# Block products for the second product of a second pair of token tiles, with its block weights made ahead

## Chip, cores and metric

One NeuronCore of a Trainium2 chip runs the whole program. The metric is the device time in microseconds (us) of one execution; the median of the runs shown counts.

## What is computed

Linear attention with an RMS norm feeds two MLPs, all in float32. There are 4608 tokens, a model width of 512, and inner widths of 2048 and 768.

```python
kv  = einsum('bhsd,bhse->bhde', k, v)          # 8 batches, 8 heads, 576 tokens, head size 64
out = einsum('bhsd,bhde->bhse', q, kv)
x   = out / sqrt(mean(out*out) + 1e-6) * g_norm
g   = s * maximum(x @ w_in, 0)**2 + b          # first MLP:  512 -> 2048 -> 512
x   = g @ w_out
h   = maximum(maximum(x @ w1, x @ w2), x @ w3) # second MLP: 512 -> 768 -> 512
y   = h @ w_out2
```

## The kernel before

Every operand of a matmul is held as a high and a low part, and a product is three matmuls (high by high, high by low, low by high) that add up in a PSUM bank. ScalarE makes the high part by a copy, VectorE the low part by a subtraction. Tokens come in nine tiles of 512. Tiles 0 to 2 go through the first MLP in the classic form, beside attention. Tiles 3 to 8 go in three pairs, `PAIRS` = (3,4), (5,6), (7,8), called pair 1, 2 and 3 here (`s` = 0, 1, 2 in the code). Then the second MLP takes the tiles in super steps of one or two tiles.

**Block products.** Two tiles and two row chunks of a weight make a 2 by 2 block matrix, which is multiplied with seven block products instead of eight (`A11` to `S4`, `t1` to `t4`; products p1 to p7, later ones add to the bank of an earlier one after ScalarE has copied it). The first product of every pair (`h_steps`, eight steps `q` of 42 matmuls, 336 in all) and the whole second MLP (`v1`, nine block products; `Output`) have this form. The second product of the first MLP is classic in pairs 1 and 2: while step `q` of the first product runs, the four output chunks of tile `ta` take the gated rows of step `q - 1` (192 matmuls), rows of tile `tb` are stored to DRAM (`g_dr`), and class `Second` multiplies them afterwards (192 more, the run part). Only pair 3, `BLOCK_Y`, has it in block form, in class `Blocks` (line 1687): `beside` multiplies b11 and b21 beside the steps (96 matmuls), `sink` (1711) makes the operands t1 to t4 of a step by four subtractions on VectorE, `early` and `ready` load and split them, and `run` (1781) multiplies the five other products, eight each (240 matmuls).

**Weights.** `block_op(q)` (1630) adds high and low of two chunks of `w_out`, forms four combinations, splits them (four copies of 128x256 on ScalarE; two 128x512 and eight 128x256 operations on VectorE) and stores four results and one old block to `ws_dr`. The eight run beside the first product of pair 3. `fetch` (1699) brings them back, seven blocks (1792 KB) a time, into the two buffers `wa`; the last five go into a tile of their own, `cp`. `com_op(i)` makes the combined weights of block product i of the second MLP from two raw chunks (`fused`: on ScalarE two Abs, two scalings and four copies; on VectorE sixteen operations) and stores 1792 KB to `wc_dr[i]`; `out_op` does the same for the last product. Before, com_op 0 runs in the plain stage (line 1484), 1 and 2 beside tile 2 (1541), 3 in pair 1, 4 to 7 and `out_op(2)` in pair 2, and out_op 0, 1 and com_op 8 inside the first super step of the second MLP (1910).

**What sets the order.** The kernel is written as one program; `tick` counts matmuls, and `beside_of(fns, a, b)` spreads side work (attention for the next pair, weight operations, loads of the next tokens) evenly over a range of that count. A string such as "L....hr.hrs.ab..e..." says at which of equal steps a weight operation loads, computes and stores. `in_order` puts an instruction behind the main work's last one on its engine. From there a scheduler orders ready instructions of each engine; in the second MLP matmuls are tied to program order. All loads and stores go through SP's queue, in order, and `store` delays one by some ticks. A pool such as `wpo` (16 tiles for `w_out`) or `wa` (two) gives a tile again once its last reader is through.

Of the kernel before, what the change touches and what calls it, by code (L numbers as in the profile page):

```python
# [10 lines left out]
F32 = mybir.dt.float32  # L11
# [11 lines left out]
P = 128  # L23
# [48 lines left out]
def fused_kernel(ctx, tc, qt, kv, kvr, g_norm, w_in, w_out, s, b, w1, w2, w3, w_out2, out):  # L72
# [72 lines left out]
    BLOCK_Y = {len(PAIRS) - 1}  # L145
    ws_dr = dram.tile([5 * QF, P, 2, HW], F32, name="ws_dr")

# [422 lines left out]

    def four(nm):
        return w2p["p"].tile([P, 2 * DM], U32, tag="p", name=nm)

    def work(nm):
        return w2p["p"].tile([P, 2 * DM], U32, tag="p", name=nm)
# [26 lines left out]
    def fused(srcs, turned, target, dst, raws=None, tabs=wide, his=hi_tile):  # L602
# [59 lines left out]
        if target:  # L662
            def both(k):
                to_hi(k + 1)
                to_lo(k)

            fns += [partial(to_hi, 0), partial(both, 0), partial(both, 1), partial(to_lo, 2), end]
        else:
            fns += [partial(to_hi, *range(4)), partial(to_lo, *range(4)), end]
# [188 lines left out]
    def v1(si, q, w):  # L858
# [49 lines left out]
        a = copy(bank("a"), x)  # L908
        d = bank("d")
# [559 lines left out]

    def com_op(i, here=False, **homes):  # L1470
# [8 lines left out]
    homes = {  # L1479
        "raws": lambda: rawp.tile([P, 2 * DM], U32, tag="raw", name="raw"),  # L1480
        "tabs": lambda: [wt1.tile([P, DM], U32, tag="ta", name="tab") for _ in range(2)],
        "his": lambda: stage().bitcast(F32R).rearrange("p (n c) -> p n c", c=HW),
    }
    early = phased(com_op(0, **homes), "L.h.r.h.rs.a.b.e")
# [56 lines left out]
    seq = [fn for i in (1, 2) for fn in phased(com_op(i, **homes), "L..hrhrs.ab.e..")]  # L1541
    beside_of(seq, 0, 5 * len(seq))
# [87 lines left out]
    def block_op(q):  # L1630
        got = {}

        def sums():
            got["raw"], got["com"] = raw, com = blocks(four("F")), blocks(work("G"))
            for i in range(2):
                hi, lo = (wo[2 * q + i][:, z].bitcast(F32).rearrange("p (n c) -> p n c", c=HW) for z in range(2))
                nc.vector.tensor_tensor(out=raw[:, 2 * i:2 * i + 2], in0=hi, in1=lo, op=ALU.add)

            def tt(o, x, y, op):
                nc.vector.tensor_tensor(out=com[:, o], in0=x, in1=y, op=op)  # L1640

            tt(0, raw[:, 1], raw[:, 3], ALU.add)
            tt(1, com[:, 0], raw[:, 0], ALU.subtract)
            tt(2, raw[:, 2], com[:, 1], ALU.subtract)
            tt(3, raw[:, 0], raw[:, 1], ALU.subtract)

        def his():
            own = got["raw"].bitcast(F32R)
            for k in range(4):
                t = w2p["f"].tile([P, 2, HW], F32R, tag="f", name="ws") if k < 2 else own[:, 2 * k - 4:2 * k - 2]  # L1650
                got[k] = t
                nc.scalar.activation(out=t[:, 0], in_=got["com"][:, k], func=ACTF.Copy)

        def los():
            for k, to in enumerate((2, 0, 4, 1)):
                t = got[k]
                nc.vector.tensor_tensor(out=t[:, 1], in0=got["com"][:, k], in1=t[:, 0].bitcast(F32), op=ALU.subtract)
                store(ws_dr[to * QF + q], t.bitcast(F32), 12)
            with tc.issue_after(behind[0]):
                dma(out=ws_dr[3 * QF + q], in_=wo[2 * q + 1][:, :, HW:].bitcast(F32))  # L1660

        return [partial(tied_in, fn) for fn in (sums, his, los)]

# [23 lines left out]
    class Blocks:  # L1687


        def __init__(self, ta, tb):  # L1690
            self.ta, self.tb = ta, tb
# [3 lines left out]
            for q in range(QF):  # L1695
                self.w["b11", q], self.w["b21", q] = wo[2 * q], wo[2 * q + 1]
            self.made = 0

        def fetch(self, c):
            ks = list(range(7 * c, min(7 * c + 7, 5 * QF)))  # L1700
            if len(ks) == 7:
                t = wc_tile("wa").rearrange("p a b c -> p (a b c)").rearrange("p (k z c) -> p k z c", z=2, c=HW)
                got = [(ks, t)]
            else:
                got = [(ks, w2p["cp"].tile([P, 5, 2, HW], F32R, tag="hl", name="ws"))]
            for k, t in got:
                dma(out=t.bitcast(F32), in_=ws_dr[k[0]:k[-1] + 1].rearrange("k p z c -> p k z c"))
                for i in range(len(k)):
                    self.w[self.order[k[i]]] = t[:, i]

        def sink(self, q):
            r = self.raw
            a, b = ((wpo if q else w2p["g4"]).tile([P, 2, DM], F32, tag="w", name="ops") for _ in range(2))
            for nm, t in (("t1", a[:, 0]), ("t2", a[:, 1]), ("t3", b[:, 0]), ("t4", b[:, 1])):
                r[nm, q] = t

            def sub(nm, x, y):
                nc.vector.tensor_tensor(out=r[nm, q], in0=x, in1=y, op=ALU.subtract)

            def sink(i, j, x):  # L1720
# [13 lines left out]
        def early(self, cnt):  # L1734
            r = self.raw
            for nm, q in self.order[:cnt]:
# [44 lines left out]
        def run(self):  # L1781
            for k, e in enumerate(self.order):
# [230 lines left out]
```

## Time and profile before

| | us |
|---|---|
| median of 3 runs (1382.25 to 1385.03) | 1382.88 |
| the profiled execution: span, first to last instruction | 1383.6 |
| the profiled execution: its own time | 1385.45 |
| PE busy (matmuls) | 1358.9 |
| VectorE (DVE) busy | 986.8 |
| ScalarE (ACT) busy | 786.9 |

PE is TensorE's matmuls and PEld its weight loads, which overlap them; DVE is VectorE, ACT is ScalarE, and SP issues the transfers. The profile names a group of instructions by line, engine, operation and tiles, out<-in. The granted clock of TensorE was 0.998 of full speed on average, so every stretch here is at the level of 2.4 GHz.

### The profile page before, as it was taken

Reading aid. Unit: us, or ns where it says so; the run is one execution under the profiler, and the core shown is the slowest. Engines: PE = TensorE matmul, PEld = TensorE weight load, DVE = VectorE, ACT = ScalarE, POOL = GpSimd, SP = SyncE. Lnnn points to the kernel's source line nnn. Section 1 sums busy time; section 2 is a strip of 40 time slices with the busy share of each in tenths; the row PEclk is TensorE's granted clock in tenths of the full one; section 3 lists DMA queues with packets and bytes.
Section 4 is the critical chain, followed back from the end, with each engine's and each line's share of the span. In section 5 each row is a group of like instructions: output and inputs, shape, how many; then the busy total and the mean of one; then the engine's idle time right before and its main releaser. Section 6 shows DMA issues by size and latency. Waiting matters only on the chain.

```text
span 1383.6 us, 19615 instructions
## 1 busy us (share of the span) xinstructions
PE 1358.9 (98%) x6822; PEld 1122.2 (81%) x6822; DVE 986.8 (71%) x1878; ACT 786.9 (57%) x1538; POOL 10.6 (1%) x40
## 2 busy tenths in 40 slices
PE   8999999999999999999999999999999999999998
PEld 6878788787888888877887777887998888888886
DVE  8998887878767676678767676786684674666555
ACT  7975666666777657677466774444453442443332
POOL 1000000000000000000000000000000000000000
PEclk9999999999999999999999999999999999999999
DMA  8486647786666676786767979647865554563532
GB/s 305 127 250 210 213 146 224 258 294 233 242 241 233 202 298 225 270 303 221 278 219 245 325 261 332 239 157 260 307 236 173 199 197 152 185 249 114 176 144 62
DMA packets 140458, 311.43 MB, mean 225 GB/s; under 512 B 50118, under 2 KB 71750, under 8 KB 131398
## 3 DMA queue, kind: packets, MB, share of 16 engines
q1 hardware_dynamic: 140352, 310.17, 64.4%
q8 instruction: 54, 0.88, 0.3%
q14 instruction: 46, 0.38, 0.1%
q10 hardware_dynamic: 6, 0.00, 0.0%
HBM read 218.89 MB, written 91.23 MB: 224 GB/s over the span
## 4 chain that ended last, share of the span: by engine, by line
PE 76%; DMA 9%; DVE 8%; ACT 3%; issue 2%; SPq 1%; DVEq 0%; ACTq 0%
PE x L524 19%; PE y L524 16%; PE d L524 12%; PE o L524 9%; PE b L524 6%; PE a L524 6%; PE h L449 2%; DVE tb L155 2%; DMA wc_dr<-raw 1%; PE h L155 1%; DMA wq<-wo_dr 1%; PE ops L369 1%; DMA raw<-in_w_out 1%; PE y L155 1%; PE kvps L347 1%
## 5 line engine op out<-in xcount | busy, mean ns | idle before, releaser
L524 PE MATMUL y<-gh,w 128*128 128x512 f32 x720 | 236.6, 391 | 0.9 <-ACT gh L506 0.9
L524 PE MATMUL d<-t,wc 128*128 128x512 f32 (+1 forms) x828 | 199.5, 376 | 0.0
L524 PE MATMUL x<-t,wc 128*128 128x512 f32 (+1 forms) x828 | 199.3, 376 | 0.0
L524 PEld LDWEIGHTS d<-t,wc 128*128 128x128 f32 x828 | 148.7, 188 | 27.9
L524 PEld LDWEIGHTS x<-t,wc 128*128 128x128 f32 x828 | 148.4, 188 | 27.6
L524 PEld LDWEIGHTS y<-gh,w 128*128 128x128 f32 x720 | 135.1, 188 | 28.6 <-ACT gh L506 1.3
L524 PE MATMUL y<-gl,w 128*128 128x512 f32 x360 | 141.0, 392 | 0.7 <-DVE gl L507 0.7
L873 DVE TENSOR_TENSOR c<-d,u 128x512 f32<-128x512 f32 (+1 forms) x45 | 28.7, 637 | 116.3 <-PE d L524 115.8
L524 PE MATMUL x<-b,wc 128*128 128x512 f32 (+1 forms) x414 | 100.1, 377 | 2.5 <-DVE r L490 1.7
L524 PE MATMUL b<-b,wc 128*128 128x512 f32 (+1 forms) x414 | 100.3, 378 | 0.0
L524 PE MATMUL a<-b,wc 128*128 128x512 f32 (+1 forms) x414 | 100.3, 376 | 0.0
L524 PEld LDWEIGHTS x<-b,wc 128*128 128x128 f32 x414 | 74.2, 188 | 17.5 <-DVE r L490 2.7
L524 PEld LDWEIGHTS b<-b,wc 128*128 128x128 f32 x414 | 73.8, 188 | 15.7 <-ACT b L809 2.2
L524 PEld LDWEIGHTS a<-b,wc 128*128 128x128 f32 x414 | 74.3, 188 | 13.8
L524 PEld LDWEIGHTS y<-gl,w 128*128 128x128 f32 x360 | 67.7, 188 | 13.7 <-DVE gl L507 1.1
L524 PE MATMUL o<-t,wq 128*128 128x512 f32 (+1 forms) x354 | 75.5, 369 | 0.0
L155 PE MATMUL h<-xh,w 128*128 128x512 f32 (+1 forms) x216 | 73.3, 383 | 1.0 <-ACT r L155 0.9
L868 ACT ACTIVATE a<-x 128x512 f32<-128x512 f32 (+1 forms) x45 | 24.3, 539 | 86.5 <-PE x L524 86.4
L524 PEld LDWEIGHTS o<-t,wq 128*128 128x128 f32 x354 | 62.4, 188 | 11.2
L868 ACT ACTIVATE b<-x 128x512 f32<-128x512 f32 (+1 forms) x45 | 24.3, 539 | 77.2 <-PE x L524 77.2
L155 PE MATMUL y<-gh,w 128*128 128x512 f32 (+1 forms) x200 | 65.1, 371 | 0.8 <-ACT st L155 0.8
L507 DVE SCALAR_TENSOR_TENSOR gl<-r,cst,gh 128x512 fp32r<-128x512 f32 x56 | 41.9, 749 | 32.8 <-ACT gh L506 32.3
(243 smaller groups left out, 2679.0 us busy)
## 6 DMA issues: line engine op xcount, KB each, us to landing
wc<-wc_dr SPq DMA_DIRECT2D x44, 1792.0 KB, 7.5
wc<-wp_dr SPq DMA_DIRECT2D x16, 1792.0 KB, 8.3
kv<-in_kv SPq DMA_DIRECT2D x32, 512.0 KB, 5.7
wp_dr<-wc SPq DMA_DIRECT2D x8, 1792.0 KB, 6.7
raw<-in_w_out SPq DMA_DIRECT2D x23, 512.0 KB, 5.0
gb<-g_dr SPq DMA_DIRECT2D x46, 256.0 KB, 5.9
g_dr<-r SPq DMA_DIRECT2D x43, 256.0 KB, 2.2
y_dr<-st SPq DMA_DIRECT2D x42, 256.0 KB, 2.8
```

Of the source, the lines that this page charges most:

```text
L155: tail[eng] = call(*args, **kw).ins
L347: nc.tensor.matmul(pb[d, i * D:(i + 1) * D], lhsT=t[:, 0, d], rhs=t[:, 1, d], start=(c == 0), stop=(c == NC))
L369: nc.tensor.matmul(pb, lhsT=l, rhs=r, start=(i == 0), stop=(i == 2))
L449: nc.tensor.matmul(h[:, :n], lhsT=w[:, z, kk, :], rhs=x[:, kk, o:o + n], start=(i == 0), stop=(i == 3 * KD - 1))
L507: nc.vector.scalar_tensor_tensor(out=gl, in0=r, scalar=b, in1=gh.bitcast(F32), op0=ALU.add, op1=ALU.subtract).ins,
L524: ins = nc.tensor.matmul(*args, **kw)
L868: main["act"] = nc.scalar.activation(out=out, in_=pb, func=ACTF.Copy).ins
L873: main["dve"] = nc.vector.tensor_tensor(out=o, in0=pb, in1=t, op=ALU.add).ins
```

## The change

Pair 2 joins pair 3 in `BLOCK_Y`. The eight block-weight operations move from pair 3 to earlier stages: 0 and 1 in the plain stage, 2 to 5 beside tile 2, 6 and 7 in the run part of pair 1. They also store the blocks b11 and b21 to `aw_dr`, from which pair 3 loads them again, since pair 2's operands take the places of `w_out`. The operations of the second MLP's weights move back: com_op 0 to pair 1, 1 and 2 to pair 2, 3 to 6 and out_op 2 to pair 3, 7 and 8 into the first super step, where a product now has seven places for side work instead of six. In pair 2 the four operands of the first step have no tiles that last; they go to DRAM (`op_dr`) and are loaded again. All 40 blocks now come through the two buffers `wa` (5 first, then 7 a time), and the first loads of what follows wait for a free one. In a block pair the side work must end with the first product (`T`). A second pool, `p2`, holds side work in pair 3. The core of the diff:

```diff
-    BLOCK_Y = {len(PAIRS) - 1}
+    BLOCK_Y = {len(PAIRS) - 2, len(PAIRS) - 1}
+    aw_dr = [dram.tile([P, 2, 2, HW], F32, name=f"aw_dr{q}") for q in range(QF)]
+    op_dr = [dram.tile([P, TW], F32, name=f"op_dr{i}") for i in range(4)]
...
     def four(nm):
-        return w2p["p"].tile([P, 2 * DM], U32, tag="p", name=nm)
+        taken[0] += 1
+        more = "p2" in w2p and taken[0] % 5 > 2
+        return w2p["p2" if more else "p"].tile([P, 2 * DM], U32, tag="p", name=nm)
...
         a = copy(bank("a"), x)
+        go()
         d = bank("d")
...
+        def end():
+            for k, to in enumerate((2, 0, 4, 1)):
+                dma(out=ws_dr[to * QF + q], in_=got[k].bitcast(F32))
+            with tc.issue_after(behind[0]):
+                for i in range(2):
+                    dma(out=aw_dr[q][:, :, i], in_=wo[2 * q + i][:, :, :HW].bitcast(F32))
+                dma(out=ws_dr[3 * QF + q], in_=wo[2 * q + 1][:, :, HW:].bitcast(F32))
...
-    early = phased(com_op(0, **homes), "L.h.r.h.rs.a.b.e")
+    early = [fn for q in range(2) for fn in phased(block_op(q, **taus), ".shl.e..")]
...
-    seq = [fn for i in (1, 2) for fn in phased(com_op(i, **homes), "L..hrhrs.ab.e..")]
-    beside_of(seq, 0, 5 * len(seq))
+    seq = [fn for q in range(2, 6) for fn in phased(block_op(q, **taus), ".shl.e..")]
+    beside_of(seq, 0, 6 * len(seq))
...
+        def weights(self, q):
+            if q < QF and ("b11", q) not in self.w:
+                t = wpo.tile([P, 2, DM], F32R, tag="w", name="w2")
+                with tc.issue_after(behind[0]):
+                    dma(out=t.bitcast(F32).rearrange("p z (i c) -> p z i c", i=2), in_=aw_dr[q])
+                self.w["b11", q], self.w["b21", q] = t[:, :, :HW], t[:, :, HW:]
+
+        CUTS = (0, 5, 12, 19, 26, 33, 40)
+
         def fetch(self, c):
...
+            a, e = self.CUTS[c:c + 2]
+            t = wc_tile("wa").rearrange("p a b c -> p (a b c)").rearrange("p (k z c) -> p k z c", z=2, c=HW)[:, :e - a]
+            with tc.issue_after(behind[0]):
+                dma(out=t.bitcast(F32), in_=ws_dr[a:e].rearrange("k p z c -> p k z c"))
...
+                own = [fpool("op") for _ in names]
+                self.away.update({(nm, q): op_dr[i] for i, nm in enumerate(names)})
...
             def sub(nm, x, y):
-                nc.vector.tensor_tensor(out=r[nm, q], in0=x, in1=y, op=ALU.subtract)
+                nc.vector.tensor_tensor(out=here[nm], in0=x, in1=y, op=ALU.subtract)
+                if (nm, q) in self.away:
+                    store(self.away[nm, q], here[nm], 8)
...
-                if k % 7 == 0 and 0 < k < 35:
...
+                if k in self.CUTS[1:5]:
+                    self.fetch(self.CUTS.index(k) + 1)
+                elif k == self.CUTS[5]:
+                    following(0)
...
+            following(1)
             self.out("b", self.tb, 0)
...
+        T = V + 12 * QF if blk else V + U
         if s + 1 < len(PAIRS):
-            beside_of(rare_steps(*groups[5 + s]), 0, V + U - 10)
+            beside_of(rare_steps(*groups[5 + s]), 0, T - 10)
         if s == 1:
-            ops = [com_op(i) for i in range(4, NQ - 1)] + [out_op(KC - 1)]
-            beside_of([fn for op in ops for fn in phased(op, "L....hr.hrs.ab..e...")], 0, V + U - 12)
+            beside_of([fn for i in (1, 2) for fn in phased(com_op(i), "L....hr.hrs.ab..e...")], 0, T - 12)
         if s == 2:
...
+            ops = [com_op(i) for i in range(3, NQ - 2)] + [out_op(KC - 1)]
+            beside_of([fn for op in ops for fn in phased(op, "L....hr.hrs.ab.e..")], 0, T - 12)
...
-                beside_of(phased(com_op(3), "L....hr.hrs.ab..e"), 20, 20 + 17 * 9)
+                beside_of(phased(com_op(0), "L....hr.hrs.ab..e"), 20, 20 + 17 * 9)
...
+        if s == 0:
+            beside_of([fn for q in (6, 7) for fn in phased(block_op(q), "shl..e..")], 115, U - 12)
...
-    ops = [out_op(0, True), out_op(1, True), com_op(NQ - 1, True)]
-    inside += [fn for op in ops for fn in phased(op, "L...hr.hrs.aaabe")]
+    ops = [out_op(0, True), out_op(1, True), com_op(NQ - 2, True), com_op(NQ - 1, True)]
+    inside += [fn for op in ops for fn in phased(op, "L..hr.hrs.aaab")]
```

## Rows read from the trace of the kernel before

**Rows 1.** Page, first part: engine, busy time, share of the span, instructions

```profile
PE 1358.9 (98%) x6822; PEld 1122.2 (81%) x6822; DVE 986.8 (71%) x1878; ACT 786.9 (57%) x1538; POOL 10.6 (1%) x40
```

**Rows 2.** Timeline of PE, begin of the second MLP: start, length, group

```profile
856.24 1.52 PE L524 MATMUL x<-b,wc 128*128 128x512 f32 x6
857.60 1.52 PE L524 MATMUL d<-t,wc 128*128 128x512 f32 x6
```

**Rows 3.** Timeline of PE, borders of pair 2, pair 3 and its run part

```profile
508.88 1.52 PE L524 MATMUL x<-b,wc 128*128 128x512 f32 x6
...
518.87 1.52 PE L524 MATMUL d<-t,wc 128*128 128x512 f32 x6
...
696.47 1.52 PE L524 MATMUL x<-b,wc 128*128 128x512 f32 x6
...
799.86 0.50 PE L524 MATMUL x<-gh,wc 128*128 128x512 f32 x1 [0.36 <-ACT keep L548]
```

**Rows 4.** Timeline of PE, attention's matmuls in pair 1 and pair 2

```profile
454.86 1.39 PE L347 MATMUL kvps<-kv 128*64 128x64 f32 x40
...
643.33 0.30 PE L369 MATMUL ops<-qh,kvbd 128*128 128x320 f32 x1
...
643.77 0.39 PE L524 MATMUL y<-gh,w 128*128 128x512 f32 x1
```

**Rows 5.** Waits of weight loads, 697 to 798: total, times, longest

```profile
PEld x L524 <- DVE r L490: 2.7, 3, 1.8
...
PEld b L524 <- ACT b L809: 1.7, 7, 0.4
```

**Rows 6.** Stretches: us, busy PE, PEld, DVE, ACT, POOL, clock, DMA share, GB/s

```profile
336.00:353.00 17.00, 17.00 (x78) 13.78 (x77) 12.40 (x22) 14.06 (x29) 0.00 (x0) 1.00 0.38 136
335.00:473.00 138.00, 138.00 (x767) 113.43 (x766) 94.89 (x180) 100.11 (x204) 2.41 (x8) 1.00 0.61 215
483.00:494.00 11.00, 11.00 (x50) 9.09 (x50) 10.88 (x21) 8.12 (x15) 0.00 (x0) 1.00 1.03 412
505.00:519.00 14.00, 14.00 (x64) 11.64 (x63) 8.61 (x14) 6.84 (x13) 0.00 (x0) 1.00 0.41 156
519.00:653.00 134.00, 131.66 (x661) 107.44 (x660) 98.46 (x202) 96.27 (x193) 0.61 (x2) 1.00 0.72 256
697.00:800.00 103.00, 100.64 (x432) 79.45 (x431) 70.62 (x139) 73.37 (x134) 0.00 (x0) 1.00 0.76 265
800.00:857.00 57.00, 56.02 (x244) 45.51 (x245) 43.50 (x69) 34.49 (x59) 0.00 (x0) 1.00 0.88 307
857.00:935.00 78.00, 78.00 (x346) 64.59 (x345) 59.74 (x121) 35.99 (x61) 0.00 (x0) 1.00 0.59 215
```

**Rows 7.** Groups of ACT, 516 to 655, the last 697 to 798: busy, mean ns, idle

```profile
L194 ACT ACTIVATE tab<-raw 128x512 f32<-128x512 f32 x10 | 6.7, 667 | 2.3 <-DMA raw<-in_w 1.4 <-DMA raw<-in_w_out 0.8 <-DVE raw L213 0.2
...
L409 ACT ACTIVATE y<-mps,cst 128x320 f32<-128x320 f32 (+1 forms) x12 | 6.1, 507 | 5.0 <-PE mps L407 4.9
...
L371 ACT ACTIVATE sq<-ops 128x320 f32<-128x320 f32 (+1 forms) x11 | 4.5, 413 | 1.5 <-PE ops L369 1.5
...
L643 ACT ACTIVATE hi<-raw 128x512 fp32r<-128x512 f32 x5 | 3.2, 631 | 4.0 <-DVE raw L213 4.0
...
L1652 ACT ACTIVATE ws<-G 128x256 fp32r<-128x256 f32 x16 | 6.2, 411 | 5.8 <-DVE G L1640 5.8
```

**Rows 8.** Groups of DVE, 516 to 655, the last two 697 to 798

```profile
L412 DVE SCALAR_TENSOR_TENSOR t<-t,y 128x320 f32<-128x320 f32 (+1 forms) x12 | 5.6, 465 | 0.2
...
L1637 DVE TENSOR_TENSOR F<-w 128x512 f32<-128x512 f32 x14 | 9.0, 683 | 0.0
...
L1657 DVE TENSOR_TENSOR ws<-G,ws 128x256 fp32r<-128x256 f32 x16 | 6.2, 416 | 0.0
```

**Rows 9.** DMA issues, whole span: count, size, median us to landing

```profile
wc<-ws_dr SPq DMA_DIRECT2D x5, 1792.0 KB, 8.6
...
ws<-ws_dr SPq DMA_DIRECT2D x1, 1280.0 KB, 10.7
```

More of the change, by code (lines that the diff above doesn't have):

```diff
@@ L665, in both, with close @@
                 to_lo(k)
[L667 removed]
+            def close():
+                to_lo(2)
+                end()
+            fns += [partial(to_hi, 0), partial(both, 0), partial(both, 1), close]
         else:
@@ L1477, in com_op @@
         return fused([chunk(ws[jb], mb), chunk(ws[ja], ma)], False, target if here else None, wc_dr[i], **homes)
[L1479 to L1483, printed above, removed]
-    early = phased(com_op(0, **homes), "L.h.r.h.rs.a.b.e")
+    taus = {"raws": lambda: rawp.tile([P, 2 * DM], U32, tag="raw", name="raw"), "ws": lambda: wt1.tile([P, DM], U32, tag="ta", name="ws").bitcast(F32R).rearrange("p (z c) -> p z c", z=2)}
+    early = [fn for q in range(2) for fn in phased(block_op(q, **taus), ".shl.e..")]
     todo, span, k_done, base = [], 1, 0, 0
@@ L1628, in out_op @@
         return fused([chunk(w_out2, 2 * c + k) for k in range(2)], True, target if here else None, wo_dr.get(c))
[L1630 to L1662, printed above, removed]
     prep.todo += [pair_op(i) for i in range(QF)]
@@ L1687, in fused_kernel, with __init__ @@
     class Blocks:
-        def __init__(self, ta, tb):
-            self.ta, self.tb = ta, tb
+        def __init__(self, ta, tb, first):
+            self.ta, self.tb, self.heads = ta, tb, None
+            self.away = {("b22", q): g_dr[tb][q] for q in range(QF)}
             self.raw, self.op, self.w = {}, {}, {}
@@ L1694, in __init__ @@
             self.order = [(nm, q) for nm in ("t2", "t3", "t1", "t4", "b22") for q in range(QF)]
-            for q in range(QF):
+            for q in range(QF if first else 0):
                 self.w["b11", q], self.w["b21", q] = wo[2 * q], wo[2 * q + 1]
             self.made = 0
-        def fetch(self, c):
[L1700 to L1709, printed above, removed]
+        def weights(self, q):
[4 more added lines that the diff above has]
+                self.w["b11", q], self.w["b21", q] = t[:, :, :HW], t[:, :, HW:]
@@ L1714, in sink @@
-            for nm, t in (("t1", a[:, 0]), ("t2", a[:, 1]), ("t3", b[:, 0]), ("t4", b[:, 1])):
-                r[nm, q] = t
+            names = "t1", "t2", "t3", "t4"
+            if q or self.heads:
+                own = []
+                for _ in range(2):
+                    t = (wpo if q else self.heads).tile([P, 2, DM], F32, tag="w", name="ops")
+                    own += [t[:, 0], t[:, 1]]
+            else:
+                own = [fpool("op") for _ in names]
+                self.away.update({(nm, q): op_dr[i] for i, nm in enumerate(names)})
@@ L1735, in early @@
             r = self.raw
-            for nm, q in self.order[:cnt]:
-                if nm == "b22" and (nm, q) not in r:
-                    r[nm, q] = fpool("b22")
-                    dma(out=r[nm, q], in_=g_dr[self.tb][q])
+            for e in self.order[:cnt]:
+                if e in self.away:
+                    r[e] = fpool("op")
+                    dma(out=r[e], in_=self.away.pop(e))
         def ready(self, cnt):
@@ L1846, in fused_kernel @@
                 blk.fetch(0)
-            if blk and q == 0:
-                fns = [fn for f in range(QF) for fn in [*block_op(f), none, none, none]]
-                beside_of(fns, 3, (QF - 1) * (V + 12 * (QF - 1)) // QF)
+            if blk:
+                blk.weights(q + 2)
+                if end:
+                    blk.early(2)
             steps = h_steps(w, toks[s], q, blk.sink(q) if blk else split_sink(tb, q, gates), blk is not None)
```

77 lines of the change are left out of this document (55 added, 22 removed).

## Prediction

> **What bounds the kernel now.** I read the page's first part, then the stretches of the two first-MLP stages that the change alters, then TensorE's timeline at their borders, and last the waits and the groups of single engines inside them. The page has PE busy for 98% of the span [rows 1]; no other engine comes near that. But a busy share is no rate: matmuls overlap, so one is reported longer than the step to the next. The step is read from starts: a group of six matmuls of 128x512 begins at 856.24 and the next at 857.60, 1.36 us or 0.2267 us each [rows 2]. Removed matmuls are priced by that step, not by their mean duration.
>
> The borders [rows 3]: pair 2 (tiles 5 and 6) begins with the product at 508.88, pair 3 (tiles 7 and 8) with the one at 696.47, and the second MLP at 856.24 [rows 2]. Behind 508.88 the scheduler has put 36 matmuls of pair 1 (the d product follows only at 518.87), 36 x 0.2267 = 8.2 us. Pair 2 thus takes 187.6 - 8.2 = 179.4 us. Its work: 336 matmuls of the first product and 2 x 192 of the second, 720 x 0.2267 = 163.2 us, and the attention steps beside it: 80 small ones at 1.39 us for 40, and 60 (12 items x 5) at the step of (643.77 - 643.33)/3 = 0.147 us [rows 4], 2.8 + 8.8 = 11.6 us. It loses 179.4 - 163.2 - 11.6 = 4.6 us. Pair 3, which already multiplies by seven block products, takes 159.8 us for 672 matmuls, 152.3 us: it loses 7.4 us, 5.5 of them before 799.86 and 2.0 behind. That is the model of what pair 2 becomes. What it loses is named in the waits of that stretch: weight loads wait 2.7 us for r of VectorE (the x bank must be emptied first) and 1.7 us for the copy b of ScalarE [rows 5].
>
> **The change, part by part.**
>
> *Second product of pair 2.* Two classic tiles of 192 matmuls become seven products of 8 x 6 = 336: 48 fewer, 48 x 0.2267 = **-10.9 us**. If pair 2 then loses what pair 3 loses, 7.4 instead of 4.6, 2.8 us go back. PE is the bound, so the difference arrives at the end unless another engine takes over.
>
> *ScalarE in the first part of pair 2.* This is the cost I am least sure of. In the block form the squares of p2 and p3 go to ScalarE. Pair 3's first part has ScalarE busy 73.4 us of 103 [rows 6]. From this go the 8 block-weight operations of 4 copies at 0.41 us (13.1), and to it come 12 attention items of six instructions between 0.41 and 0.51 us (12 x 6 x 0.46 = 33.1) and two weight operations of eight instructions, four like the 0.67 us row, the others 0.41 to 0.63 (5.0 each, 10.0) [rows 7]. Sum 103.4 us. PE there has 432 x 0.2267 + 11.6 = 109.5 us: ScalarE would be at 94%, where pair 3 stands at 71% and pair 2 now at 96.3 of 134 [rows 6]. The first part shrinks under an engine whose work doesn't. The attention's steps, spread up to T - 10, have 422 matmuls instead of 518 to lie beside. Bounds for the extra loss: 0, since a slice of pair 1 has ScalarE busy 14.06 of 17 us, 83%, and PE without a gap [rows 6], to 10, if 83% is also the most that it reaches (103.4/0.83 = 124.6 us, against 109.5 + 5.5). I take **+2**, nearer the low end: PE's order is made by a scheduler that puts ready work first (the first product of pair 2 stands before 36 matmuls of pair 1 [rows 3]), and each step has four small block products that can stand before one that waits. VectorE: 70.6 - 37.6 (8 operations of 2 x 0.68 + 8 x 0.42 us) + 27.9 (attention, 12 x 5 x 0.465) + 17.1 (two weight operations of 8.5 us: 7 x 0.68, 9 x 0.42) = 78 us [rows 6, 8], 71%, not a bound.
>
> *Operands without a home.* The first block row's four operands go to DRAM and come back: 4 stores and 4 loads of 256 KB on SP's queue in a stage that loses 8 gate stores and 8 gate loads of the same size. Costed at nothing: the loads are asked for nine block products ahead, the first one when the last step begins; without that cover it is one landing of a few microseconds.
>
> *Pair 3.* Block-weight operations (13.1 us ScalarE, 37.6 VectorE) go; four weight operations and the output one come (25 and 43 us). ScalarE goes to 85 of 103 us, VectorE to 76. Eight weight tiles of 512 KB come back from DRAM two steps ahead, one a step, behind what SP has queued; hidden by those two steps. Taken **+1**, bounds 0 and +4 by the same argument as above.
>
> *Earlier stages.* Six block-weight operations stand where three weight operations stood in the plain stage and tile 2's first product: VectorE 6 x 4.7 against 3 x 8.5 us, ScalarE less by 5, transfers 6 x 1.8 MB, all stores, against 3 x 2.8 MB, of which 1.0 loaded. SP gets seven DMAs at the end of each, all of finished tiles; the loads of x and of attention stand behind them. Taken 0, bounds -1 and +1. Operations 6 and 7 come into the last third of pair 1's run part, 9.4 us more on VectorE, whose stretch 505 to 519 has 8.6 us busy of 14 [rows 6]: **+0.3**, bounds 0 and +3; late next would be the splits of pair 2's operands.
>
> *Second MLP.* One more weight operation in the first super step, 8.5 us on VectorE, which has 59.7 of 78 us busy in the six block products from 857 [rows 6]; one load of 1792 KB less. Seven slots a product instead of six put the last piece of the ninth block's weights behind the end of the eighth product, and its second product reads it 1.36 us later. **+0.5**, bounds -0.5 and +3.
>
> Sum: -10.9 + 2.8 + 2 + 1 + 0.3 + 0.5 = **-4.3 us**. It is made on the profiled execution (span 1383.6, its own time 1385.45), which lies 2.6 us above the median of 1382.88; the edit's difference is carried to the median: 1382.88 - 4.3 = **1378.6**.
>
> **Rivals.**
>
> *A, slower: ScalarE becomes the bound of pair 2's first part.* Place: between the first p1 of pair 2 and its first t2 product. For it: 103.4 us of work in 109.5; the copies a and b gate matmuls, ScalarE works in order, and the attention's instructions stand among them. Against it: the slice at 83% without a gap. Price: 124.6 us instead of 116.9, so -4.3 + 7.7 = +3.4, **1386.3**. It decides from a first part of about 121 us, at which nothing is left of the gain.
>
> *B, no change: the transfers bind the run parts.* Before, the last five block weights had a tile of their own; now all 40 pass two buffers, seven at a time, each fetch issued when a buffer falls free and wanted 7 x 6 x 0.2267 = 9.5 us later. A fetch of 1792 KB lands after 8.6 us by its median, the smaller one took 10.7 [rows 9]. If pair 2's five land after 10.7 too, each is 1.2 us late: +6, **1384.6**. Against it: pair 3's run part lost only 2.0 us in all at 307 GB/s, and the slice 483 to 494 moved 412 GB/s with PE busy 11.00 of 11 us [rows 6]. With four more operands of 256 KB, pair 2's run part would want about 18.5 MB in 57 us, 325 GB/s, 79% of that slice. The Trainium skill, "DMA: Bandwidth & Descriptors", section Bandwidth, gives the HBM side of a core as about 358 GB/s; by that the run part would stand at 91% of its limit and I would give this rival 0.4. The slice of 412 GB/s disagrees with that figure as a ceiling, and the measurement decides.
>
> *C, more: all covers hold* as in pair 1, where PE is busy 138.00 of 138.00 us beside the same attention work [rows 6]. Then pair 2 loses no more than now and the rest is free: -10.9, **1372.0**.
>
> **How the numbers follow.** A measurement of this kernel can tell about 0.2%, 2.8 us, from no change. Forecast (1375 to 1380): 0.43. C: 0.15; the matmuls are gone for certain, but block products carry waits that the classic form hasn't. B, or enough of A to eat most of the gain: 0.25. A: 0.17. So faster 0.43 + 0.15 = 0.58, same 0.25, slower 0.17. The range runs from C, 1372.0, to a little above A, 1387.0; outside are A at its worst with the bounds of pair 3 and the second MLP (+4 and +3), and a gain in which even earlier stages win.
>
> **What would show it.** The page after: the y groups lose 384 matmuls, the products on ws_dr's and the kept weights gain 336. Pair 2 from its first product to pair 3's should take about 173 us (A: 181, C: 168.5). Its first part about 117 us; ScalarE's busy share there near 88%. A is shown by PE waits for a, b (L809) or r on ScalarE adding up to over 10 us in it, B by PE waits for ws_dr or wp_dr of over 1 us each at blocks 5, 12, 19, 26 or 33, or at the first product of pair 3. Pair 3 should take 160 to 162 us, the first super step no more than 1 us longer. I am wrong if pair 2 takes over 178 us, or if time is lost where I costed nothing: the earlier stages, pair 1's run part, or the weights of the last two blocks of the second MLP's first super step.

## The result, and the profile after

The changed kernel takes 1392.82 us (median of 7 runs, 1388.05 to 1399.44) against 1384.1 for the kernel before in the same series (1382.25 to 1386.4): ratio 1.0061, 95% interval 1.0038 to 1.0084. It is slower by some 8 us, where 4.3 us less were forecast. The profiled execution has a span of 1391.0 us (own time 1393.11), 7.4 more than the 1383.6 before.

First part of the page of the kernel after: engine, busy time, share of the span, instructions; it answers to [rows 1].

```profile
PE 1356.8 (98%) x6774; PEld 1113.2 (80%) x6774; DVE 1012.2 (73%) x1920; ACT 815.6 (59%) x1582; POOL 10.7 (1%) x40
```

The 48 matmuls are gone: 6774 instead of 6822. PE's busy time fell by only 2.1 us, and VectorE and ScalarE have 25 and 29 us more. PE still stands at 98%: this line alone would not show where the kernel became slower.

Timeline of PE, kernel after, at the borders: begin of pair 2, its run part, pair 3, its run part, second MLP. Columns: start, length, group.

```profile
510.85 1.52 PE L526 MATMUL x<-b,wc 128*128 128x512 f32 x6
...
520.83 1.52 PE L526 MATMUL d<-t,wc 128*128 128x512 f32 x6
...
634.92 0.50 PE L526 MATMUL x<-gh,wc 128*128 128x512 f32 x1 [2.04 <-ACT keep L550]
...
693.01 1.52 PE L526 MATMUL x<-b,wc 128*128 128x512 f32 x6
...
800.99 0.63 PE L526 MATMUL x<-gh,wc 128*128 128x512 f32 x1
...
860.43 1.52 PE L526 MATMUL x<-b,wc 128*128 128x512 f32 x6
```

Beside [rows 2, 3]. Pair 2 lasts 693.01 - 510.85 - 8.2 = 174.0 us (the same 36 matmuls of pair 1 stand behind its first product); before it was 179.4: **-5.4**. Pair 3 lasts 860.43 - 693.01 = 167.4 instead of 159.8: **+7.6**, 4.6 of them before its run part and 3.1 in it. Pair 1 began later by **+1.9** (its first copy a of L818 at 338.27, before at 336.33) and took as long as before. The first super step, from its first copy a to that of the next, took 118.7 instead of 115.4: **+3.3**. What follows is equal. 1.9 - 5.4 + 7.6 + 3.3 = +7.4, all of the difference of the spans.

Stretches of the kernel after: from:to, us, busy PE, PEld, DVE, ACT, POOL, granted clock, DMA share, GB/s.

```profile
510.90:634.90 124.00, 121.40 (x609) 96.77 (x607) 90.51 (x175) 100.33 (x200) 0.61 (x2) 1.00 0.74 259
634.90:693.00 58.10, 56.23 (x240) 44.69 (x241) 45.51 (x72) 36.69 (x60) 0.00 (x0) 1.00 0.92 320
693.00:802.00 109.00, 103.24 (x437) 81.74 (x436) 82.65 (x158) 84.01 (x142) 0.00 (x0) 0.98 0.80 293
802.00:860.00 58.00, 55.45 (x237) 45.11 (x236) 42.27 (x66) 33.22 (x56) 0.00 (x0) 0.97 0.90 309
790.00:805.00 15.00, 10.73 (x40) 8.02 (x39) 13.63 (x29) 9.97 (x17) 0.00 (x0) 0.89 0.48 170
805.00:815.00 10.00, 7.51 (x27) 5.82 (x26) 4.83 (x8) 3.14 (x5) 0.00 (x0) 0.84 0.99 350
815.00:860.00 45.00, 44.94 (x198) 36.81 (x197) 34.44 (x54) 28.64 (x49) 0.00 (x0) 1.00 0.87 302
```

Pair 2 has ScalarE busy 100.33 of 124 us, 81%. In pair 3, VectorE stands at 76% and ScalarE at 77%, with the room that the forecast had read as cover; yet PE stands idle 109 - 103.24 = 5.8 us in the first part and 2.5 in the second, and the granted clock fell, which it did not before [rows 6]. The last three rows place it: 25 us, from 790 to 815, hold 4.3 + 2.5 us of idle PE and the clocks 0.89 and 0.84; the 45 us behind have neither.

Waits of PE in the kernel after, 692 to 864: what it waited for, total, times, longest.

```profile
PE w L526 <- ACT gh L508: 4.4, 2, 4.1
PE x L526 <- DMA wc<-ws_dr: 2.5, 1, 2.5
PE x L526 <- ACT gh L508: 0.7, 1, 0.7
```

These are 7.6 us. Before, PE waited 3.1 us in pair 3: 0.7 for ws_dr, 0.7 for others, and, in the kernel before:

```profile
PE x L524 <- DVE r L490: 1.7, 2, 1.4
```

The 4.5 us more, and some 3.3 us that the lower clock costs (last section), make about 7.8, all of the +7.6.

The first wait after the change is for gh, which ScalarE makes of r, which VectorE makes. Timeline of all engines, kernel after, end of pair 3's first product.

```profile
791.27 0.89 DVE L206 SCALAR_TENSOR_TENSOR tab<-raw,tab 128x128 uint32<-128x128 uint32 x4
...
791.78 1.58 PE L526 MATMUL b<-b,wc 128*128 128x512 f32 x6
792.08 0.42 DVE L212 TENSOR_SCALAR tab<-raw 128x512 uint32<-128x512 uint32 x1
792.53 0.76 DVE L215 CUSTOM_DVE_ANT_0 raw<-tab 128x512 uint16<-128x512 uint16 x2
...
793.33 0.76 DVE L704 TENSOR_TENSOR tab<-raw 128x256 f32<-128x256 f32 x2
...
794.00 0.42 DVE L704 TENSOR_TENSOR tab<-tab,raw 128x256 f32<-128x256 f32 x1
794.34 0.68 DVE L492 CUSTOM_DVE_ANT_0 r<-d,u 128x512 f32<-128x512 f32 x1
...
795.92 1.32 ACT L487 ACTIVATE r<-r,cst 128x512 f32<-128x512 f32 x2
797.15 0.71 ACT L508 ACTIVATE gh<-r,cst 128x512 fp32r<-128x512 f32 x1
...
797.91 0.60 PE L526 MATMUL w<-gh,w 128*128 128x512 f32 x1 [4.08 <-ACT gh L508]
...
800.14 0.63 PE L526 MATMUL w<-gl,w 128*128 128x512 f32 x1
800.57 0.63 PE L526 MATMUL w<-gh,w 128*128 128x512 f32 x1
...
810.74 0.47 PE L526 MATMUL x<-gh,wc 128*128 128x512 f32 x1 [2.48 <-DMA wc<-ws_dr]
```

From 791.27 to 794.34 VectorE does the pieces of the output's weight operation (L206, L212, L215, L704), and the sum r of the last step stands behind them. It starts 5.3 us after its product d has ended (789.00); without the side work (e2) the same sum starts 0.8 us after its product (787.82 and 788.63). ScalarE gets r late, PE gets gh late and stands 4.08 us. Behind that, matmuls of L526 start 0.43 us apart (800.14, 800.57), twice their usual step: the clock is down for some 3 us.

The second wait is for the second piece of the block weights. The first piece lasts for five blocks only, and the second was issued late. Timeline of SP, which issues the transfers, kernel after:

```profile
799.27 0.92 SPq L163 DMA_DIRECT2D wo_dr<-tab  x2
800.81 0.72 SPq L163 DMA_DIRECT2D wo_dr<-raw  x1
801.62 0.39 SPq L163 DMA_DIRECT2D wc<-ws_dr  x1
```

The last product that reads the buffer's old contents (b<-b,wc, from 791.78) ended at 793.36. So the load went out 8 us after its buffer was done with, directly behind the stores of the output's weight operation, and 0.6 us after the run part had begun (800.99).

Waits of PE behind that, 860 to 985: the first super step of the second MLP.

```profile
PE o L526 <- DMA wq<-wo_dr: 3.3, 1, 3.3
PE x L526 <- DVE c L882: 0.7, 1, 0.7
PE d L526 <- DVE wc L653: 0.2, 1, 0.2
```

### The profile page after: what moved, and what is told of

Its sections match the earlier page's. It is cut to its first block, busy times and chain, and to the rows that moved or that the text cites. A ratio compares the mean times of both kernels' runs of the same rounds, so it can differ in the third digit from the quotient of the medians.

```text
span 1391.0 us, 19600 instructions
## 1 busy us (share of the span) xinstructions
PE 1356.8 (98%) x6774; PEld 1113.2 (80%) x6774; DVE 1012.2 (73%) x1920; ACT 815.6 (59%) x1582; POOL 10.7 (1%) x40
## 4 chain that ended last, share of the span: by engine, by line
PE 78%; DVE 8%; DMA 7%; ACT 4%; issue 2%; SPq 0%; DVEq 0%; ACTq 0%
PE x L526 19%; PE d L526 13%; PE y L526 11%; PE o L526 9%; PE b L526 7%; PE a L526 6%; PE h L451 5%; PE y L157 3%; PE h L157 3%; DMA y<-x_dr 2%; PE ops L371 1%; PE kvps L349 1%; DMA wq<-wo_dr 1%; DVE tb L157 1%; PE w L526 1%
## 5 line engine op out<-in xcount | busy, mean ns | idle before, releaser
L526 PE MATMUL d<-t,wc 128*128 128x512 f32 (+1 forms) x828 | 200.5, 377 | 0.2 <-DVE wc L653 0.2
L526 PE MATMUL x<-t,wc 128*128 128x512 f32 (+1 forms) x828 | 200.5, 376 | 0.0
L526 PEld LDWEIGHTS d<-t,wc 128*128 128x128 f32 x828 | 148.1, 188 | 28.3 <-DVE wc L653 0.6
L526 PEld LDWEIGHTS x<-t,wc 128*128 128x128 f32 x828 | 148.3, 188 | 27.6 <-DVE t L183 0.2
L526 PE MATMUL y<-gh,w 128*128 128x512 f32 x464 | 153.3, 394 | 0.4 <-ACT gh L508 0.4
L526 PEld LDWEIGHTS y<-gh,w 128*128 128x128 f32 x464 | 87.6, 190 | 18.8 <-ACT gh L508 1.1
L526 PE MATMUL b<-b,wc 128*128 128x512 f32 (+1 forms) x414 | 100.9, 379 | 0.5 <-ACT b L818 0.3
L526 PE MATMUL x<-b,wc 128*128 128x512 f32 (+1 forms) x414 | 100.0, 377 | 1.3 <-DVE c L882 0.7
L526 PE MATMUL a<-b,wc 128*128 128x512 f32 (+1 forms) x414 | 100.3, 376 | 0.0
L526 PE MATMUL y<-gl,w 128*128 128x512 f32 x232 | 91.4, 394 | 0.2 <-DVE gl L509 0.2
L526 PEld LDWEIGHTS x<-b,wc 128*128 128x128 f32 x414 | 74.2, 188 | 16.9 <-DVE c L882 1.3
L526 PEld LDWEIGHTS b<-b,wc 128*128 128x128 f32 x414 | 73.6, 188 | 17.5 <-ACT b L818 4.1
L526 PEld LDWEIGHTS a<-b,wc 128*128 128x128 f32 x414 | 74.4, 188 | 13.9
L877 ACT ACTIVATE a<-x 128x512 f32<-128x512 f32 (+1 forms) x45 | 24.3, 539 | 88.0 <-PE x L526 88.0
L526 PE MATMUL o<-t,wq 128*128 128x512 f32 (+1 forms) x354 | 75.5, 369 | 0.0
L526 PEld LDWEIGHTS o<-t,wq 128*128 128x128 f32 x354 | 62.4, 188 | 11.2
L877 ACT ACTIVATE b<-x 128x512 f32<-128x512 f32 (+1 forms) x45 | 24.3, 539 | 71.7 <-PE x L526 71.7
L451 PE MATMUL h<-xh,w 128*128 128x512 f32 x192 | 64.2, 392 | 0.0
L487 ACT ACTIVATE r<-r,cst 128x512 f32<-128x512 f32 x80 | 57.3, 720 | 11.6 <-DVE r L492 10.0
```

Of the source, the lines that this page charges most:

```text
L451: nc.tensor.matmul(h[:, :n], lhsT=w[:, z, kk, :], rhs=x[:, kk, o:o + n], start=(i == 0), stop=(i == 3 * KD - 1))
L487: main["act"] = nc.scalar.activation(out=out, in_=src, func=ACTF.Square, scale=root).ins
L526: ins = nc.tensor.matmul(*args, **kw)
L877: main["act"] = nc.scalar.activation(out=out, in_=pb, func=ACTF.Copy).ins
```

## Experiments

Each kernel is the changed one with the edit shown, except the first. Only the core of an edit is shown: where an operation is left out, finished weights of the same size are read in its place. "Intervals" are the times between the first copies a of pair 2, pair 3 (L809 before, L818 after), the first super step and the one behind it (L868 before, L877 after). Pair 2's holds the 8.2 us of pair 1. The ratio is of all runs; the intervals are of one profiled execution each, which for e10 took 3.9 us and for e2 2.4 us more than the kernel's median, for e4 3.0 and for e5 2.9 less.

| kernel | ratio to before | pair 2 | pair 3 | first super step |
|---|---|---|---|---|
| before / again | 1 | 187.2 / 186.7 | 159.8 / 160.4 | 115.4 / 115.5 |
| after | 1.0061 | 182.2 | 167.4 | 118.7 |
| e1 pair 2 classic | 1.0044 | 183.7 | 163.5 | 117.4 |
| e2 no side work in pair 3 | 0.9983 | 182.4 | 155.1 | 119.4 |
| e3 seven blocks first | 1.0061 | 185.6 | 163.9 | 118.4 |
| e4 output's operation first | 1.0056 | 183.0 | 164.5 | 118.4 |
| e5 no operation 7 | 1.0049 | 182.5 | 166.6 | 115.3 |
| e6 side work spread on | 1.0089 | 183.7 | 164.5 | 123.4 |
| e7 squares on VectorE | 1.0061 | 181.9 | 165.2 | 120.0 |
| e8 no output's operation | 1.0037 | 181.7 | 162.4 | 120.6 |
| e9 a tile of their own | 1.0062 | 182.4 | 165.2 | 120.0 |
| e10 e9, e4, one op moved | 1.0060 | 186.9 | 167.6 | 115.2 |
| e11 no side work in pair 2 | 1.0031 | 177.8 | 164.8 | 119.9 |

Where the code of pair 3 is the same (after, e5, e7, e11), its interval is 164.8 to 167.4. Its instructions stand in the same order in after, e5 and e7 (in e11 but for the last tenth), so this is mostly the difference of one execution from another. An interval of one profile is good to about 1.3 us.

### The kernel before, again

The kernel before, unchanged.

> The kernel before, profiled once more, to see how far one profiled execution stands for another. Pair 1 should begin within 1.5 us of the first profile (first copy a at 336.3 us). If it does, the 2 us that the changed kernel has lost by then are the change's; the profiles of kernels with the same early stages lay at 335.1 to 339.2.

One run gave 1384.26 us, and the intervals are within 0.6 us of those before: the profile of before can be relied on.

### Pair 2 classic, the weight operations where the change put them

```diff
-    BLOCK_Y = {len(PAIRS) - 2, len(PAIRS) - 1}
+    BLOCK_Y = {len(PAIRS) - 1}
```

> Against the changed kernel (1392.8 us): pair 2 multiplies its second product in the classic form again, everything else stays moved. Theory 1 (the loss sits in pair 3, where five weight operations now stand beside the products): pair 2 takes 179 to 181 us instead of 182, less the matmuls of pair 1 behind its first product, pair 3 stays at 163 to 168 us, the total rises by about 5 us to 1398. Theory 2 (the loss is the traffic that the block form of pair 2 brings, kept blocks loaded again and operands through DRAM): pair 3 falls back to about 160 us and the total stays at 1392 or falls.

1389.28 us, ratio 1.0044 (1.0029 to 1.0058). Stretch of this kernel in pair 2, columns as above:

```profile
520.00:650.00 130.00, 130.00 (x661) 108.00 (x659) 78.64 (x147) 85.70 (x171) 0.62 (x2) 1.00 0.66 227
```

With two weight operations instead of five beside it, PE has no gap in 130 us, and classic pair 2 takes 183.7 - 8.2 = 175.5 us. Theory 1 had pair 3 right (163.5); its 179 to 181 for pair 2 and its total of 1398 did not come out. The block form beside the same two takes 174.0, and 173.5 to 175.5 in the other kernels with the same code of pair 2 (e2, e4, e5, e6, e8, e9). So of the 10.9 us of removed matmuls 1.5 arrive by the kernel after, 0 to 2 by all seven; the larger part of pair 2's 5.4 came from operations that left it. Pair 3 takes 163.5 here, with a wait of 3.6 us for the same gh: with the block form in pair 2 it is 1.3 to 3.9 us longer, where its kept blocks are loaded again and the DMA share of its first 97 us is 0.85 instead of 0.72. Which of the two does it, no run separates.

### Side work out of pair 3, and out of pair 2

```diff
-            ops = [com_op(i) for i in range(3, NQ - 2)] + [out_op(KC - 1)]
+            ops = []
```

> The five weight operations of pair 3 are left out (the second MLP reads other finished weights of the same size in their place, so its traffic stays). Theory 1: pair 3 falls from 167.4 to 157 to 161 us, the total by 7 to 9 us to 1384 to 1386. Theory 2 (fetches of block weights and the two buffers): pair 3 stays at 164 or more, the total falls by 3 us at most.

1380.58 us, ratio 0.9983 (0.9972 to 0.9993). Stretch and waits of PE of this kernel, pair 3:

```profile
694.00:791.00 97.00, 96.89 (x423) 78.44 (x422) 42.21 (x63) 62.29 (x97) 0.00 (x0) 1.00 0.56 204
```

```profile
PE x L526 <- DMA wc<-ws_dr: 0.4, 1, 0.4
```

Without the five operations pair 3 takes 155.1 us, against 164.8 to 167.4 with them: 2.2 us for one, by the mean of 166.0. The wait for gh goes, and of the one for ws_dr 0.4 us are left, though its fetches are the same. The second piece is issued in time here. Timeline of SP and of PE, this kernel:

```profile
792.50 0.37 SPq L163 DMA_DIRECT2D wc<-ws_dr  x1
...
793.93 0.39 PE L526 MATMUL x<-gh,wc 128*128 128x512 f32 x1
```

That is 0.2 us behind the last product that reads the buffer (it ended at 792.28) and 1.4 us before the run part begins, where the kernel after was 0.6 us behind it: these 2.0 us are about the difference of the two waits (2.5 and 0.4). The total is 2.4 us below the kernel before. Even with five weight operations for nothing, the change would gain no more. The eight block-weight operations of before cost 159.8 - 155.1 = 4.7 together, 0.6 each, with 37.6 us of VectorE and 13.1 of ScalarE. The five have 43 us of VectorE, little more, but 25 of ScalarE, and cost more than twice as much. The edit takes out the operations' loads and stores too (DMA share 0.56 where it was 0.85), so what their engine time costs and what their transfers cost, this run does not separate.

```diff
-            beside_of([fn for i in (1, 2) for fn in phased(com_op(i), "L....hr.hrs.ab..e...")], 0, T - 12)
+            beside_of([fn for i in () for fn in phased(com_op(i), "L....hr.hrs.ab..e...")], 0, T - 12)
```

> Pair 2's two weight operations (com_op 1 and 2) are left out (finished weights of the same size are read in their place); attention and the block products stay. If side work is what keeps the block form of pair 2 from paying, pair 2 falls from 182 to 177 to 179 us (172 + 8 would be without any loss), the total by 3 to 5 us to 1388 to 1390. If the block form loses by its own chain of copies and sums beside attention, pair 2 stays at 181 or more and the total within 2 us.

1386.65 us, ratio 1.0031 (1.0017 to 1.0045). Pair 2 takes 177.8 instead of 182.2: 4.4 us for two, again 2.2 for one. In the classic form it was less: 179.4 us with five [rows 3], 175.5 with two in e1, which is 3.9 for three, 1.3 each. Against its matmuls (152.3 + 11.6 = 163.9 us) block pair 2 loses 10.1 us with the two operations and 5.7 without; classic pair 2 in e1 lost 0.7 (175.5 - 174.8). So the block form costs by itself, and each operation costs more beside it. Its first product also leaves the operations a shorter stretch; whether form or length makes them dearer, no run separates.

### Which operation in pair 3, and where

The output's operation left out, then put first, then all five spread into the run part:

```diff
-            ops = [com_op(i) for i in range(3, NQ - 2)] + [out_op(KC - 1)]
+            ops = [com_op(i) for i in range(3, NQ - 2)]
```

> Of pair 3's five weight operations only the last, out_op, is left out (other weights of the same size are read in its place). If the time follows the amount of work, a fifth of the 12 us goes: total about 1390, pair 3 about 165. If it is out_op's place and its long VectorE operations at the last step, the wait of 4.1 us goes with the low clock behind it: pair 3 160 to 163, total 1386 to 1388.

1387.67 us, 1.0037 (1.0024 to 1.0050). The wait of 4.1 us is gone and pair 3 is 5.0 us shorter than in the kernel after (3.6 than the mean of 166.0), which is more than the 2.2 to 2.5 of a fifth of the work, though by little more than the 1.3 of an interval; the wait for ws_dr stays at 2.8.

```diff
-            ops = [com_op(i) for i in range(3, NQ - 2)] + [out_op(KC - 1)]
+            ops = [out_op(KC - 1)] + [com_op(i) for i in range(3, NQ - 2)]
```

> The operation for the last product's weights (out_op) is the first of the five in pair 3 instead of the last. Theory 1a (its VectorE instructions at the last step stand before the sums that empty the banks): the wait of 4.1 us at the end of the first part goes, pair 3 falls to 162 to 164 us, the total by 3 to 5 us. Theory 1b (it is the sum of the work, not which operation stands where): a wait of the like stays, total within 1.5 us.

1391.87 us, 1.0056 (1.0040 to 1.0072). Waits of PE in this kernel, 692 to 864:

```profile
PE x L526 <- DMA wc<-ws_dr: 2.4, 1, 2.4
PE x L526 <- ACT gh L508: 1.4, 1, 1.4
PE w L526 <- ACT gh L508: 1.4, 2, 1.1
PE x L526 <- DVE gl L509: 0.8, 1, 0.8
```

The long wait splits into small ones for the same chain. Pair 3 gains 2.9 us in this execution, which is within what executions differ by (167.4 to 164.8); the total does not move by more than can be told. Neither expectation is borne out in full.

```diff
-            beside_of([fn for op in ops for fn in phased(op, "L....hr.hrs.ab.e..")], 0, T - 12)
+            beside_of([fn for op in ops for fn in phased(op, "L....hr.hrs.ab.e..")], 0, T + 220)
```

> The five weight operations of pair 3 are spread over its first product and its run part instead of the first product alone. Theory 1 (VectorE and ScalarE are too full in the first part, so that their instructions come late for the products): pair 3 falls from 164 to 167 us to 159 to 161, the total by 4 to 6 us to about 1387. Theory 2 (it is the sum of the work in the pair, or transfers): no change within 2 us.

1395.97 us, 1.0089 (1.0076 to 1.0102). This is slower, where 1387 was expected. The 4.1 us are gone here too, but the work now lies in the run part: in 692 to 985 PE waits 2.2 and 0.4 us for ws_dr, 1.6 for gl, and in the second MLP 3.3 for c on VectorE and 3.1 for wq; the first super step takes 123.4.

### The fetch of the block weights

```diff
-        CUTS = (0, 5, 12, 19, 26, 33, 40)
+        CUTS = (0, 7, 14, 21, 28, 35, 40)
```

> The first fetch of block weights takes seven blocks instead of five, as before the change, the last one five. Theory 1: the wait for ws_dr of 2.5 us in pair 3's run part goes, the run part falls from 59.4 to about 57 us, the rest stays: total 1390. Theory 2: all run parts gain, the total falls by 5 us or more. If the later loads now come late instead, no gain.

1392.68 us, 1.0061 (1.0047 to 1.0075). Waits of PE in this kernel, 692 to 864:

```profile
PE w L526 <- ACT gh L508: 4.5, 2, 4.1
PE x L526 <- DMA wc<-wp_dr: 1.8, 1, 1.8
PE x L526 <- DMA wc<-wc_dr: 0.8, 1, 0.8
```

With seven blocks first the wait for ws_dr is gone, but the last piece has five, and the loads behind it (wp_dr, wc_dr) become late by as much. Pair 2 got longer by 3.4, so nothing is gained.

A tile of their own for the first five, in place of the pool `p2`, so that the next fetch goes out one buffer earlier:

```diff
-            t = wc_tile("wa").rearrange("p a b c -> p (a b c)").rearrange("p (k z c) -> p k z c", z=2, c=HW)[:, :e - a]
+            if c == 0 and "cp" in w2p:
+                t = w2p["cp"].tile([P, 5, 2, HW], F32R, tag="hl", name="ws")
+            else:
...
-            w2p["p2"] = pool("prep2", 2, st=mlp1)
+            w2p["cp"] = pool("cp", 1, st=mlp1)
```

> In pair 3 the first five block weights get a tile of their own again (in place of the second pool for side work), and the fetches behind them are issued one buffer earlier. If the two buffers cost time there, the wait for ws_dr of 2.5 us and the low clock behind it go: run part 56 to 57 us instead of 59.4, total 1389 to 1390. If the second pool for side work was worth more than that, pair 3's first part grows and the total stays or rises.

1390.98 us, 1.0062 (1.0047 to 1.0077). Run part of pair 3 and waits of PE, 692 to 864, in this kernel:

```profile
802.00:860.00 58.00, 58.00 (x252) 47.79 (x251) 44.54 (x71) 34.96 (x59) 0.00 (x0) 0.98 0.86 295
```

```profile
PE w L526 <- ACT gh L508: 4.1, 1, 4.1
PE x L526 <- DVE r L492: 2.4, 1, 2.4
```

The run part is without a gap. The first part, whose side work has three tiles instead of five, waits 2.4 us more for r.

### Operation 7 of the first super step

```diff
-    ops = [out_op(0, True), out_op(1, True), com_op(NQ - 2, True), com_op(NQ - 1, True)]
-    inside += [fn for op in ops for fn in phased(op, "L..hr.hrs.aaab")]
+    ops = [out_op(0, True), out_op(1, True), com_op(NQ - 1, True)]
+    inside += [fn for op in ops for fn in phased(op, "L....hr..hr.s.aaab")]
```

> In the first super step of the second MLP the operation for the eighth block product's weights is left out; other finished weights of the same size are loaded in its place (the three others are spread evenly over the places). If that operation is what costs time there, the super step falls from 118.7 us (first copy a to the next super step's) to about 115.5 and the total by about 3 us. If the wait for the last product's weights (3.3 us, a load beside two others of 1792 KB) is the cause, the super step stays above 117.

1389.59 us, 1.0049 (1.0035 to 1.0063). The first super step takes 115.3 us, as before: the operation costs 3.4 there. By the ratios the total fell by 1.7 us, less than can be told from nothing.

### Squares on VectorE

In pair 2 the squares of p2 and p3 go back from ScalarE to VectorE:

```diff
-            steps = h_steps(w, toks[s], q, blk.sink(q) if blk else split_sink(tb, q, gates), blk is not None)
+            steps = h_steps(w, toks[s], q, blk.sink(q) if blk else split_sink(tb, q, gates), s == 2)
```

> In pair 2 the squares of two of the four outputs of a step go back to VectorE, as in the classic form: 16 x 0.72 us less on ScalarE, 16 x 0.75 us more on VectorE. If ScalarE bounds pair 2's first part, pair 2 falls by 3 to 6 us and the total with it, to 1387 to 1390. If it doesn't, or VectorE is as near its limit, no change within 2 us or slower.

1392.3 us, 1.0061 (1.0049 to 1.0074). Stretch of this kernel, pair 2's first part:

```profile
510.00:635.00 125.00, 123.77 (x621) 99.38 (x620) 102.63 (x197) 92.14 (x189) 0.61 (x2) 1.00 0.75 262
```

ScalarE has about 8 us less and VectorE 12 more (in a stretch 1 us longer), and pair 2 takes 181.9 instead of 182.2. Work taken off ScalarE gains nothing. As VectorE stands at 82% after that, this alone does not clear ScalarE; the waits do: in the kernel after, from 511 to 634, the only waits of PE that its view names are 0.3 us for b and 0.2 for ql.

### All that had removed a wait, together

e9's tile, the output's operation first (e4), and operation 7 moved from the super step to pair 2. Of the edit only this last part is shown:

```diff
-            beside_of([fn for i in (1, 2) for fn in phased(com_op(i), "L....hr.hrs.ab..e...")], 0, T - 12)
+            beside_of([fn for i in (1, 2, NQ - 2) for fn in phased(com_op(i), "L....hr.hrs.ab..e...")], 0, T - 12)
```

> Three remedies at once: the own tile of e9_own_tile, out_op first in pair 3, and the eighth block product's weights made in pair 2 instead of the second MLP. If the costs are separate they add up: super step 115.5 (-3), pair 3 161 (-6), pair 2 up by 1 to 2, total 1384 to 1386, about the kernel before. If it is one shortage of ScalarE and VectorE time that only moves, the total stays above 1389.

1390.6 us, 1.0060 (1.0044 to 1.0075). The super step gets its 3.5 us back (115.2), pair 2 pays 4.7 (186.9), and pair 3 takes 167.6. This execution took 3.9 us more than the median, so these lengths may be high; but by the ratio, too, nothing is gained. The costs don't add up as waits do; they move with the side work. No complete version beat the kernel before.

## Why the prediction was wrong

**Second product of pair 2**, -10.9 + 2.8 + 2: 173.3 us forecast for pair 2, 174.0 measured, first part 634.92 - 510.85 - 8.2 = 115.9 where about 117 was said. The size is right by luck, and the reason half wrong. That three weight operations leave pair 2 was not costed as a gain; at 1.3 us each it was 3.9 (e1). And the block form brought 1.5 at equal side work, not 10.9 - 4.8 = 6.1. The two errors nearly cancelled. A wait of 2.0 us for keep on ScalarE, at the begin of the run part (634.92), is part of what it lost.

**ScalarE in pair 2 and rival A.** The work was reckoned at 103.4 us; 100.33 of 124 stood there. The rival wanted a first part of 121 us or more and waits for a, b or r of over 10; the part took 115.9, and PE waited 0.3 us for b. Moving 8 us of ScalarE's work to VectorE changed nothing (e7). Rival A falls.

**Pair 3 is the step that failed:** "Taken +1, bounds 0 and +4". It became 7.6. I had set VectorE's and ScalarE's totals (76 and 85 us of 103) beside PE's time and taken what fits as covered. ScalarE's total was right (84.01 of 109). VectorE's was 6.6 low (82.65): what is left without side work was reckoned at 70.6 - 37.6 = 33.0 us, and e2 has 42.21. Yet both still left room, and e2 has 155.1 without side work: the five operations cost 10 to 12 us, and of the 7.4 that pair 3 lost before, 4.7 were its eight block-weight operations, which I had taken for a loss of the block form. What the step left out is order, in two queues. VectorE works in order: one r that stands 3 us behind pieces of a weight operation holds up ScalarE, then PE by 4.08. SP does too: the fetch at 801.62 stands behind the same operation's stores, and PE waits 2.5. That the first wait comes from that operation, e8 shows, where it is gone; e8's own last operation holds up the fetch in the same way (2.8). How much of the 10 to 12 us is engine time and how much transfers stays open.

**Second MLP**, "+0.5, bounds -0.5 and +3": +3.3 measured, 3.4 for the one added operation by e5. The same error: 59.7 of 78 us busy on VectorE was read as room. PE waits 3.3 us there for wq, the output's weights, 1.6 before and 1.1 with the operation left out (e5). The load of wq goes out behind a weight operation's store: 78.7 us into the super step (940.70), where it was 76.1 before and 75.6 in e5.

**Rival B** had the right place in pair 3 and the wrong mechanism. Bandwidth did not bind in pair 2: its run part moved 320 GB/s and waited 0.3 us for ws_dr. The rival's lead of 9.5 us holds for seven blocks; the first piece has five, 5 x 6 x 0.2267 = 6.8. And the fetch was not issued when its buffer fell free, but when SP's queue reached it: 0.6 us into the run part of pair 3, which leaves 6.2, and PE waited 2.5 us. Removed alone, that wait was made up for elsewhere (e3, e9).

**Earlier stages**, taken 0 with bounds -1 and +1: the twelve kernels with the changed early stages have pair 1's first copy a at 335.1 to 339.2, 337.5 in the mean, against 336.3 and 335.9 before. About +1.4. The traces give the place: up to 285 us the kernel after had started 23 matmuls more than the kernel before, and it lost them behind that. Stretches of the kernel after, beside tile 2, columns as above:

```profile
290.00:295.00 5.00, 2.89 (x9) 2.11 (x10) 3.02 (x6) 3.74 (x10) 0.00 (x0) 0.80 1.01 339
295.00:300.00 5.00, 5.00 (x20) 4.05 (x20) 3.02 (x7) 1.34 (x3) 0.00 (x0) 0.86 0.42 129
```

From 285 to 300 PE is busy 12.4 to 12.5 of 15 us in all twelve and 15.0 in both traces of before, and in ten of the twelve the granted clock falls there. In the kernel after PE waits 1.3 us for og on ScalarE and 1.2 for t on VectorE, both of attention. What makes these late no run took out: the cause is open. **Pair 1's run part** cost nothing that shows.

With pair 3 at +7.6 and the second MLP at +3.3, each beyond its upper bound, and +1.9 early, the gain of 5.4 is more than spent. The text named the earlier stages and the weights of the super step's last two blocks as places where it could be wrong. The first was right; for the second PE waited only 0.2 us (wc L653), and the loss came at the output's weights. It had not thought of pair 3's ordinary steps. The change as a whole fails because it needs each weight operation to be hidden wherever it is put, and beside block products one cost about 2.2 us, where it cost 1.3 beside the classic form.

## What to carry to other kernels

Side work is not hidden because its engine has idle time in total; price it by leaving one such operation out of the stage that it will stand in, for such an operation cost 1.3 us beside one form of the main work and 2.2 to 3.4 beside another. Before you cost a buffer's fetch at nothing, count the lead of each piece, the short first and last ones too, from the moment at which the queue lets it out: look at what stands before it there. And when a long wait is removed and the total stays, look at whose queue the work went to: here no repair of a wait made the kernel faster than the one before.

## What the hardware showed that was not expected

The kernel ran at a granted clock of 1.00 in every stretch shown before [rows 6]. After, two short gaps of PE in pair 3 were followed by the level of 1.2 GHz. Stretches of the kernel after, columns as above; the third lies behind the gap of 3.30 us for wq, which ended at 956.58:

```profile
798.20:801.50 3.30, 3.11 (x8) 2.23 (x8) 3.30 (x7) 2.16 (x5) 0.00 (x0) 0.50 0.61 227
811.90:815.20 3.30, 3.30 (x10) 2.56 (x9) 1.29 (x2) 1.15 (x2) 0.00 (x0) 0.50 1.06 411
956.60:985.00 28.40, 28.40 (x145) 24.39 (x146) 18.10 (x39) 11.26 (x26) 0.00 (x0) 1.00 0.49 143
```

In this execution the fall comes behind the gap, not in it: 0.3 us after the end of the gap of 4.08 us (797.91), and 1.1 us after that of 2.48 (810.74). At these clocks 2 x 3.3 x 0.50 = 3.3 us are lost on top of the 6.6 of waiting. In e4, where the first gap is split into waits of 1.4 us and less, the stretch 790 to 805 keeps 1.00, and the gap for ws_dr has its fall:

```profile
790.00:805.00 15.00, 13.11 (x56) 9.64 (x54) 13.97 (x25) 11.61 (x20) 0.00 (x0) 1.00 0.64 224
805.00:815.00 10.00, 7.62 (x27) 5.89 (x26) 4.84 (x8) 3.58 (x6) 0.00 (x0) 0.83 1.01 377
```

A long wait can thus cost more than its own length. Its length does not settle whether it does. The gap for gh, 3.5 to 4.1 us long in after, e1, e3, e5, e7, e9 and e11, had a stretch at 0.50 across its end or right behind it in all seven. Of the gaps between 2.0 and 3.3 us some had one, as that of 2.48 us here, and some had none, as the longer one of 3.30 us here (third row) and one of 2.20 us in e1.
